# A retention, mixing and gated-MLP kernel: whole-tile first loads, a seven-product last layer and a re-searched order

## The chip, the cores and the metric

One core of one Trainium2 chip. The metric is device time in microseconds (us); an interval is given where runs were repeated. Span means the time from the first to the last instruction in the profile. The engines are TensorE (PE), VectorE (DVE), ScalarE (ACT), GpSimd (POOL) and SyncE (SP), which mainly issues transfers.

## What is computed

Three blocks follow one another on an array of 2 batches x 768 tokens x 512 features, all in float32:

```
attention: state[t] = gamma_h * state[t-1] + k[t] v[t]^T ;  y[t] = q[t] state[t] / 8     (8 heads of 64)
mixing:    theta = x @ w_theta
           u = x + w_tok_r @ (x cos theta) + w_tok_i @ (x sin theta)          (over tokens)
           x = u + relu(u @ w_ch)
gated MLP: h = gelu(x @ w_in) ;  u, v = halves of h
           v = (w_sg @ layernorm(v) * g_ln) + b_sg                             (over tokens)
           out = x + (u * v) @ w_out
```

## The kernel before, in words

**Numbers.** A float32 product is made of three passes in PE's faster type fp32r: each operand is split into a high part (ACT, line 324) and a low part (DVE, line 330), and `terms3` (line 345) issues high x high, low x high and high x low into one accumulator. A 128 x 512 tile with a contraction of 512 is thus 4 x 3 = 12 matmuls of 512 columns. Only the attention runs in plain float32.

**Tiles.** The 768 tokens of a batch are six chunks of 128; chunk i = 0 to 11 counts over both batches. From the mixing on, tokens stand in three groups of 512: group 0 is batch 0's first 512 tokens, group 1 is batch 1's, group 2 the last 256 tokens of both. Features stand in four row tiles of 128. A tile is called (group, row tile).

**Loads.** `load_half` (line 439) brings a chunk in two halves of 512 KB (q with k, and k with v). For chunk 0 each half goes in two transfers of 64 partitions, one on SP's queue and one on ACT's; all others go whole on SP's. From chunk 3 on, a load waits for the attention of the chunk three before (`gate`, line 441). Behind chunk 0's halves SP issues `dec` (line 467), 262 KB: the decay factors `dq` by which the attention's result is multiplied, and the small ones `dk` and `gone` for the keys and the state. Weights come in 1 MB transfers and are converted on ACT and DVE (`weight`, line 371).

**Attention** (`retention`, line 460): scores, a mask on DVE, a fade of v by `dk` (on ACT, eight small instructions, for the first eight chunks; else one on DVE), an outer product for the next state, the attention product, and the multiplication by `dq` on DVE.

**Last layers.** `gate_tile(g, f)` (line 961) makes the products over tokens, an affine step on DVE (line 998), a multiplication by u (line 1005), and the split into `ghl[g, f]`. `finish(g, d)` (line 1013) makes the product with `w_out` by `layer` (12 matmuls), adds x in the evacuation (line 1020) and stores. The last tile, (2, 3), is done in two halves of 256 columns (line 1057). There are 12 such tiles, 8 of them in groups 0 and 1.

**Order.** Every instruction group is an `Op` with a modelled duration, and `ORDER` (line 168) is a list found by an offline search. `Plan.schedule` (line 112) walks it with a model of the engines' and queues' times, gives out buffers and PSUM banks, and sorts by modelled start. Each engine runs its instructions in that order; a modelled gap of PE in the first 34 us is filled with matmuls on the identity (`keep_warm`, line 1137), and eight matmuls on a zeroed state come first of all.

Of the kernel before, what the change touches and what calls it, by code (L numbers as in the profile page):

```python
# [10 lines left out]
F32 = mybir.dt.float32  # L11
# [51 lines left out]
class Plan:  # L63
# [3 lines left out]
    BEGIN = {"PE": 4.9, "ACT": 2.3, "DVE": 1.4, "POOL": 2.0, "SP": 0.8, "SPA": 0.8}  # L67
    FLY = 8
# [37 lines left out]
    def switch(self, a, b):  # L106
        tiled = ("scores", "outer", "attend")
        if a in ("main", "turn") and b in tiled:
            return 0.09 if a == "main" else 0.23
        return {"attend": 0.09 * (b != "outer"), "outer": 0.07}.get(a, 0.0) * (a != b)  # L110

    def schedule(self, order):
# [8 lines left out]
        landed, last = [], {}  # L121
        for o in (self.ops[k] for k in order):
# [7 lines left out]
            if o.eng == "SP" and len(landed) >= self.FLY:  # L130
                t = max(t, landed[-self.FLY])
            for b in o.bufs:
                if b.base is None:
                    room = free[b.of]
                    b.base = min(range(len(room)), key=lambda k: room[k])
                    t = max(t, room[b.base] + 0.1)
                    room[b.base] = math.inf
            o.start, o.end = t, t + o.dur
            if o.eng in ("SP", "SPA"):
                engines[o.eng] = t + 0.45  # L140
                if sent < t + 1.25:
                    sent = t + 1.75
                    if t > 20:
                        behind = 0.4
# [4 lines left out]
                if o.eng == "SP":  # L149
                    landed.append(o.end)  # L150
# [68 lines left out]
def retention_spectral_gmlp(  # L219
# [5 lines left out]
    decays: bass.AP,  # L225
    gvec: bass.AP,
# [34 lines left out]

    ident = const.tile([P, P], F32, name="ident")
# [16 lines left out]
    dec = const.tile([P, 512 + H + NP], F32, name="dec")  # L279
    dq, dk, gone = dec[:, 0:512], dec[:, 512 : 512 + H], dec[:, 512 + H :]  # L280
    grown = const.tile([P, NP * D], F32, name="grown")
    states = [const.tile([P, NP * D], F32, name=f"state{n}") for n in range(2)]
    V.memset(states[0], 0.0)
# [19 lines left out]
    def mm(o, l, r, start, stop):  # L303
        nc.tensor.matmul(out=o, lhsT=l, rhs=r, start=start, stop=stop)  # L304
# [40 lines left out]
    def terms3(o, terms, start=True, stop=True):  # L345
        n = len(terms)
        for i, ((lh, ll), (rh, rl)) in enumerate(terms):
            mm(o, lh, rh, start and i == 0, False)
            mm(o, ll, rh, False, False)
            mm(o, lh, rl, False, stop and i == n - 1)  # L350
# [12 lines left out]
    wp = {}  # L363
# [7 lines left out]
    def weight(k, prio, eng=dve, after=()):  # L371
# [53 lines left out]
        f = lambda: words(0).bitcast(F32)  # L425
        split_hi(lambda: ap(h, F32R), f, 1024, prio, [(raw, 0), *keys], w=[h])
# [9 lines left out]

    load = {}

    def load_half(i, k):
        b, c = divmod(i, NCH)  # L440
        x = load[i, k] = Buf("pair")

        def rows(queue, a, e):
            queue.dma_start(out=ap(x)[a:e], in_=qkv[b, c, k][a:e])  # L444
# [8 lines left out]
    def landed(x):  # L453
        return [(x, "top"), (x, "low")]
# [777 lines left out]
```

## Time and profile before

| | us |
|---|---|
| median of 3 runs (375.22 to 375.40) | 375.26 |
| the profiled execution | 375.16 |
| its span | 373.4 |
| PE busy in the span | 366.1 (98%) |
| DVE busy | 267.6 (72%) |
| ACT busy | 171.8 (46%) |

The profile is of one execution. Busy times are sums over instructions; a PE that is "busy" can still run below its peak, since matmuls overlap and their ends are modelled. What counts for the time is which wait ends last in each stage.

### The profile page before, as it was taken

The page shows a single profiled execution, that of the slowest core. Times are in us where ns is not written, and L with a number is a line of the kernel's source. Part 1 is how long each engine was busy: PE and PEld are TensorE (multiplying, and loading weights), DVE is VectorE, ACT ScalarE, POOL GpSimd, SP SyncE. Part 2 cuts the span into 40 slices and gives each one's busy share as a digit, 9 for nine tenths or more (in the row PEclk, how much of TensorE's full clock was granted, in tenths as well). Part 3 has the DMA queues.
Part 4 walks back from the last instruction along what each step waited for, and adds up shares of the span by engine and source line. Part 5 has one row for each costly group of instructions (what it writes and reads, how often), then busy time and mean ns, then how long its engine had stood idle before and what let it go on. Part 6 is the DMA issues. An engine that isn't in the chain of part 4 may idle for free.

```text
span 373.4 us, 5719 instructions
## 1 busy us (share of the span) xinstructions
PE 366.1 (98%) x2372; PEld 314.1 (84%) x2372; DVE 267.6 (72%) x408; ACT 171.8 (46%) x292; POOL 11.0 (3%) x18
## 2 busy tenths in 40 slices
PE   7899999999999999999999999999999999999996
PEld 6788888888899888889988888888888888899885
DVE  1898999979887998646478237985989795542453
ACT  2877786755462576413344026427466813000010
POOL 1101002000000300000000000000000000000000
PEclk9999999999999999999999999999999999999999
DMA  7999904255438100442042000000000000000124
GB/s 214 416 409 412 366 31 145 64 216 198 168 119 326 64 0 11 190 126 100 2 149 104 2 0 0 2 0 1 2 0 0 1 2 0 30 0 2 56 85 169
DMA packets 10234, 39.04 MB, mean 105 GB/s; under 512 B 1248, under 2 KB 2272, under 8 KB 7776
## 3 DMA queue, kind: packets, MB, share of 16 engines
q1 hardware_dynamic: 10048, 38.15, 27.3%
q10 hardware_dynamic: 160, 0.52, 0.6%
q8 instruction: 18, 0.29, 0.3%
q14 instruction: 8, 0.07, 0.1%
HBM read 35.53 MB, written 3.15 MB: 104 GB/s over the span
## 4 chain that ended last, share of the span: by engine, by line
PE 94%; DMA 5%; ACTq 0%; DVE 0%; issue 0%
PE banks L304 93%; DMA b<-qkv 5%; PE banks L678 1%; ACTq L444 0%; DVE b L1057 0%
## 5 line engine op out<-in xcount | busy, mean ns | idle before, releaser
L304 PE MATMUL banks<-b,b 128*128 128x512 f32 (+2 forms) x1788 | 330.2, 351 | 0.0
L304 PEld LDWEIGHTS banks<-b,b 128*128 128x128 f32 (+1 forms) x1788 | 278.3, 183 | 46.4 <-issue 1.0
L324 ACT ACTIVATE b<-b 128x512 fp32r<-128x512 f32 (+1 forms) x61 | 50.2, 846 | 79.2 <-DVE b L1005 44.7
L330 DVE TENSOR_TENSOR b<-b,b 128x512 fp32r<-128x512 f32 (+1 forms) x61 | 56.0, 932 | 16.1 <-ACT b L324 11.9
L416 DVE SCALAR_TENSOR_TENSOR b<-b 128x1024 int32<-128x1024 int32 x32 | 39.1, 1221 | 5.0 <-ACT b L396 4.9
L819 ACT ACTIVATE b<-banks 128x512 f32<-128x512 f32 x24 | 13.5, 589 | 30.9 <-PE banks L304 30.9
L827 DVE SCALAR_TENSOR_TENSOR b<-b,banks 128x512 f32<-128x512 f32 x24 | 16.1, 682 | 15.4 <-ACT b L819 15.4
L324 ACT ACTIVATE b<-xa 128x512 fp32r<-128x512 f32 (+1 forms) x26 | 17.1, 668 | 15.3 <-DVE xa L729 8.3
L304 PE MATMUL banks<-b 64*128 64x128 f32 (+1 forms) x352 | 19.8, 261 | 2.5 <-DMA b<-qkv 2.5
L304 PEld LDWEIGHTS banks<-b 64*128 64x128 f32 (+1 forms) x352 | 17.8, 170 | 4.8 <-DMA b<-qkv 3.4
L484 DVE TENSOR_TENSOR b<-banks,causal 128x512 f32<-128x512 f32 x24 | 15.6, 684 | 8.3 <-PE banks L304 8.3
L330 DVE TENSOR_TENSOR b<-xa,b 128x512 fp32r<-128x512 f32 (+1 forms) x26 | 18.7, 730 | 2.7 <-ACT b L324 2.7
L396 ACT ACTIVATE b<-b 128x1024 f32<-128x1024 f32 x16 | 18.5, 1153 | 3.1 <-DMA b<-wts 3.1
L837 ACT ACTIVATE b<-b 128x512 f32<-128x512 f32 x24 | 14.6, 626 | 10.4 <-DVE b L827 10.3
L502 ACT ACTIVATE b<-b,dec 128x64 f32<-128x64 f32 x64 | 16.1, 336 | 5.7 <-DMA dec<-decays 5.1
L998 DVE SCALAR_TENSOR_TENSOR b<-banks,gcol,brow 128x512 f32<-128x512 f32 x12 | 8.9, 747 | 13.2 <-PE banks L304 13.2
L843 DVE SCALAR_TENSOR_TENSOR b<-b,banks 128x512 f32<-128x512 f32 x24 | 16.1, 678 | 3.0 <-ACT b L837 2.9
L686 DVE TENSOR_TENSOR b<-banks,b 128x1024 f32<-128x1024 f32 x12 | 14.5, 1219 | 0.4 <-ACT b L669 0.4
L1020 DVE TENSOR_TENSOR b<-banks,xa 128x512 f32<-128x512 f32 x8 | 5.5, 689 | 13.0 <-PE banks L304 13.0
L324 ACT ACTIVATE b<-xb 128x512 fp32r<-128x512 f32 (+1 forms) x13 | 8.4, 664 | 12.6 <-DVE xb L765 9.3
L928 ACT ACTIVATE b<-b,rstd 128x512 f32<-128x512 f32 x12 | 9.6, 806 | 7.9 <-DVE rstd L917 7.9
L634 ACT ACTIVATE b<-banks 128x512 int32<-128x512 f32 x12 | 7.1, 592 | 10.9 <-PE banks L304 10.9
(58 smaller groups left out, 179.4 us busy)
## 6 DMA issues: line engine op xcount, KB each, us to landing
b<-wts SPq DMA_DIRECT2D x16, 1024.0 KB, 4.9
b<-qkv SPq DMA_DIRECT2D x22, 512.0 KB, 10.8
out<-b SPq DMA_DIRECT2D x11, 256.0 KB, 2.4
b<-wsg SPq DMA_DIRECT2D x9, 256.0 KB, 5.5
xa<-wts SPq DMA_DIRECT2D x2, 1024.0 KB, 11.8
xb<-wts SPq DMA_DIRECT2D x1, 1024.0 KB, 9.5
b<-qkv ACTq DMA_DIRECT2D x2, 256.0 KB, 4.3
b<-qkv SPq DMA_DIRECT2D x2, 256.0 KB, 5.5
```

The lines of the kernel that those rows point to most:

```text
L304: nc.tensor.matmul(out=o, lhsT=l, rhs=r, start=start, stop=stop)
L324: act(words, lambda: A.activation(out=hi(), in_=src(), func=AF.Copy), prio=prio, r=r, **k)
L330: lambda: E.tensor_tensor(out=lo(), in0=src(), in1=hi().bitcast(F32), op=ALU.subtract),
L396: lambda: A.activation(out=words(1).bitcast(F32), in_=words(1).bitcast(F32), func=AF.Copy, scale=REBIAS),
L416: lambda scalar=scalar, op=op: V.scalar_tensor_tensor(out=words(0), in0=words(1), scalar=scalar, in1=words(0), op0=op, op1=ALU.bitwise_or,),
L484: V.tensor_tensor(out=ap(at[i])[:, h * 512 : (h + 1) * 512].rearrange("p (n t) -> p n t", n=NP), in0=ap(sc[h]).rearrange("p (n t) -> p n t ...
L502: A.activation(out=v, in_=v, func=AF.Copy, scale=dk[:, h : h + 1])
L686: V.tensor_tensor(out=z2, in0=ap(tp)[:, None, :].to_broadcast([P, 2, 512]), in1=z2, op=ALU.mult)
L819: lambda: A.activation(out=ap(s), in_=ap(t), func=AF.Square),
L827: lambda: V.scalar_tensor_tensor(out=ap(s), in0=ap(s), scalar=1.0 / GA, in1=ap(t), op0=ALU.add, op1=ALU.mult),
L837: lambda: A.activation(out=ap(s), in_=ap(s), func=AF.Tanh, scale=GA * GC),
L843: lambda: V.scalar_tensor_tensor(out=ap(o), in0=ap(s), scalar=1.0, in1=ap(t), op0=ALU.add, op1=ALU.mult),
```

## The change

**Loads.** Chunk 0's halves are loaded as the others, in one transfer of 128 partitions each on SP's queue. The table is cut in two: `dk` and `gone`, padded to 96 columns (48 KB), go on ACT's queue; `dq` (256 KB) goes on SP's. In DRAM and in the tile the halves' columns are regrouped by pairs of heads; instruction counts and sizes of the attention stay. The fade of chunk 0 moves to DVE. The wait of a load for the attention three chunks before is gone.

**Last layer.** The 8 tiles of groups 0 and 1 are one product of 2 x 2 blocks: A11, A12, A21, A22 are 256 x 256 blocks of `w_out`, transposed, and B11, B12, B21, B22 blocks of the gated activations (first index: feature half; second: batch). Winograd's form needs seven products of blocks with sums of the operands: of the weights S1 = A21 + A22, S2 = S1 - A11, S3 = A11 - A21, S4 = A12 - S2, and of the activations T1 = B12 - B11, T2 = B22 - T1, T3 = B22 - B12, T4 = B21 - T2. `seven` runs once per 128 rows of a block (j = 0, 1): seven products of 6 matmuls into four PSUM banks, `finish_four` adds and stores four tiles.

**Order.** `ORDER` is new (935 entries in place of 884). The gates now run (0,3), (0,2), (0,0), (0,1), the four of group 2, then (1,1), (1,3), (1,2), (1,0). Behind them PE does, with round j in brackets: A11 B11 [0]; tiles (2,0) and (2,2); S1 T1 [0]; tile (2,1); S2 T2 [0]; S1 T1 [1]; A12 B21 [0]; S3 T3 [0]; A11 B11 [1]; A22 T4 [0]; S2 T2 [1]; S3 T3 [1]; S4 B22 [0]; A12 B21 [1]; A22 T4 [1]; S4 B22 [1]; the two halves of (2,3). Up to the first theta product PE does the same work as before (scores of chunks 0 to 3, outer products and attention of 0 to 2). SP's queue begins: both halves of chunks 0 and 1, `dq`, the first theta weight, chunks 2 and 3, the vector `gvec`, the second theta weight, chunks 4 and 5, a `wsg` tile, the second and the first main weight, chunk 6's second half, chunk 7, chunk 10's first half, chunk 8's and chunk 6's first halves. Before, it began: chunk 0, `dec`, chunk 1, the first theta weight, chunks 2 and 3, the second theta weight, chunk 4, a `wsg` tile, chunk 5, the first main weight, chunk 6.

**The rest.** The planner's constants change, six matmuls on the zeroed state in place of eight, that state's memset first, and gaps of PE in the first 9 us filled from 0.4 us on in place of 0.8.

```diff
     def load_half(i, k):
         x = load[i, k] = Buf("pair")
-        t = dict(prio=early(i) - 12 + k, after=[gate[i - 3]] if i >= 3 else ())
-        if i == 0:
-            dma(256, lambda: rows(nc.sync, 0, 64), w=[(x, "top")], **t)
-            dma(256, lambda: rows(nc.scalar, 64, P), eng="SPA", w=[(x, "low")], **t)
-        else:
-            dma(512, lambda: rows(nc.sync, 0, P), w=[(x, "top"), (x, "low")], **t)
+        dma(
...
+            lambda: nc.sync.dma_start(out=ap(x), in_=qkv[b, c, k]),
...
         if i == 0:
-            dma(264, lambda: nc.sync.dma_start(out=dec, in_=decays), w=["dk"], prio=t - 10.9)
+            dma(48, lambda: nc.scalar.dma_start(out=dec, in_=decays), eng="SPA", w=["dk"], prio=t - 10.9)
+            dma(256, lambda: nc.sync.dma_start(out=dq, in_=qdecays), w=["dq"], prio=t - 10.9)
...
-        if i < C["FA"]:
+            if 0 < i < C["FA"]:
                 plan.op("ACT", 2.01, fade_v_heads, **k)
...
-        ghl[g, f] = pair()
-        split(ghl[g, f], lambda: ap(m), 512, prio, [m])
+        if g != 1 or f >= 2:
+            ghl[g, f] = pair()
+            split(ghl[g, f], lambda: ap(gu[g, f]), 512, prio, [gu[g, f]])
+
+    def sum_weights(base, prio):
...
+        for i, (x, y, op, of) in enumerate(pairs):
+            dve(
+                512,
+                lambda i=i, x=x, y=y, op=op: V.tensor_tensor(out=s3(i), in0=x(), in1=y(), op=op),
...
+            split(res[i], lambda i=i: ap(sums[i]), 512, prio, [sums[i]])
...
+    def sum_tokens(src, prio):
...
+            sums = [(b12, b11), (b22, own[0]), (b22, b12), (b21, own[1])]
+            for i, ((x, kx), (y, ky)) in enumerate(sums):
+                dve(
...
+                split(res[i, n], lambda i=i, t=t: ap(t[i]), 512, prio, [t[i]])
...
+    def seven(base, src, hl, ws, ts, j, prio):
+
+        z, w, x, y = (bank() for _ in range(4))
...
+        def product(o, a, b, first):
+            tile, keys = a
+
+            def products():
+                terms = [(tile(n), tuple(ap(v, F32R) for v in b[n])) for n in range(2)]
+                terms3(ap(o), terms, first, True, not first)
+
+            pe(1.36, products, r=[*keys, *b[0], *b[1]], w=[o], prio=prio)
...
+        product(z, a_of(0, 0), b_of(0, 0), True)
+        product(w, s_of(1), t_of(1), True)
+        both(u, z, w)
+        product(x, s_of(0), t_of(0), True)
+        product(y, s_of(2), t_of(2), True)
+        both(v, x, y)
+        product(z, a_of(0, 1), b_of(0, 1), False)
+        product(x, s_of(3), b_of(1, 1), False)
+        product(y, a_of(1, 1), t_of(3), False)
+        return z, x, y, u, v
...
+    def finish_four(j, ws, ts, prio):
+        z, x, y, u, v = seven(W_OUT, None, ghl, ws, ts, j, prio)
...
+        add(o, lambda: ap(z), lambda: x_tile(0, j), [z, *x_keys(0, j)], ps=True)
+        store(0, j, o, prio)
+        for g, d, part in ((1, j, x), (0, 2 + j, y)):
+            o = Buf()
+            add(o, lambda: ap(u), lambda g=g, d=d: x_tile(g, d), [u, *x_keys(g, d)])
+            add(o, lambda part=part: ap(part), lambda o=o: ap(o), [part], ps=True)
+            store(g, d, o, prio)
+        add(v, lambda: ap(u), lambda: ap(v), [u])
+        add(v, lambda: ap(v), lambda: x_tile(1, 2 + j), x_keys(1, 2 + j))
+        store(1, 2 + j, v, prio)
```

`both(o, a, b)` copies accumulator a to SBUF on ACT and adds accumulator b to it on DVE, ahead of the later products into the same banks.

## Rows read from the trace of the kernel before

**Rows 1.** Page, part 1: busy us (share of span) and instructions by engine.

```profile
PE 366.1 (98%) x2372; PEld 314.1 (84%) x2372; DVE 267.6 (72%) x408; ACT 171.8 (46%) x292; POOL 11.0 (3%) x18
```

**Rows 2.** Waits of PE, whole execution: who waited for whom: us, times, longest.

```profile
PE banks L304 <- DMA b<-qkv: 2.5, 3, 1.3
PE banks L304 <- DVE state L283: 1.3, 1, 1.3
```

**Rows 3.** Windows: stretch, length, busy us (instructions) by engine, PEclk, DMA share, GB/s.

```profile
2.00:5.00 3.00, 3.00 (x15) 2.75 (x13) 0.00 (x0) 1.28 (x1) 0.00 (x0) 1.00 1.01 249
5.00:7.50 2.50, 2.15 (x20) 1.98 (x20) 0.16 (x1) 0.00 (x0) 0.00 (x0) 1.00 0.99 204
7.50:18.60 11.10, 8.56 (x142) 7.21 (x140) 8.54 (x14) 8.88 (x27) 1.52 (x1) 1.00 1.04 417
20.00:40.00 20.00, 20.00 (x256) 16.71 (x252) 18.05 (x26) 15.95 (x44) 1.84 (x3) 1.00 1.02 409
20.00:370.00 350.00, 350.00 (x2184) 300.08 (x2178) 256.77 (x391) 160.88 (x263) 8.34 (x9) 1.00 0.24 92
300.00:340.00 40.00, 40.00 (x228) 35.30 (x227) 23.71 (x36) 6.89 (x11) 0.00 (x0) 1.00 0.02 7
300.00:370.00 70.00, 70.00 (x389) 61.33 (x387) 37.09 (x57) 9.21 (x15) 0.00 (x0) 1.00 0.11 38
```

**Rows 4.** The chain that ended last: start us, us, what.

```profile
6.55 11.99 DMA b<-qkv
18.59 11.84 PE banks L304 x146
...
143.70 226.59 PE banks L304 x1146
```

**Rows 5.** Timeline of DVE, last 10 us: start us, us, instruction [idle before, releaser].

```profile
364.72 0.69 DVE L1020 TENSOR_TENSOR b<-banks,xb 128x512 f32<-128x512 f32 x1 [4.75 <-PE banks L304]
365.33 0.68 DVE L1020 TENSOR_TENSOR b<-banks,xa 128x512 f32<-128x512 f32 x1
365.93 0.68 DVE L1020 TENSOR_TENSOR b<-banks,xb 128x512 f32<-128x512 f32 x1
...
367.44 0.69 DVE L1020 TENSOR_TENSOR b<-banks,xb 128x512 f32<-128x512 f32 x1 [0.83 <-PE banks L304]
```

**Rows 6.** Groups by line and shape, DVE and ACT: busy us, mean ns, idle before.

```profile
L330 DVE TENSOR_TENSOR b<-b,b 128x512 fp32r<-128x512 f32 x33 | 22.1, 685 | 2.3 <-ACT b L324 2.2
L998 DVE SCALAR_TENSOR_TENSOR b<-banks,gcol,brow 128x512 f32<-128x512 f32 x12 | 8.9, 747 | 13.2 <-PE banks L304 13.2
...
L324 ACT ACTIVATE b<-b 128x512 fp32r<-128x512 f32 x33 | 19.6, 623 | 44.9 <-DVE b L1005 44.7
```

**Rows 7.** Transfers from 2 to 3 us: 40 slices, and the only data queue.

```profile
GB/s 0 0 0 0 164 492 328 328 164 164 0 328 655 655 328 328 164 164 0 328 328 0 0 328 0 0 0 0 0 0 0 164 492 328 164 0 0 164 819 983
...
q10 hardware_dynamic: 51, 0.21, 87.9%
```

**Rows 8.** Timeline of the head, as rows 5.

```profile
0.78 1.20 ACTq L444 DMA_DIRECT2D b<-qkv  x2
...
0.78 1.46 SPq L444 DMA_DIRECT2D b<-qkv  x2
...
8.43 2.02 ACT L502 ACTIVATE b<-b,dec 128x64 f32<-128x64 f32 x8 [5.14 <-DMA dec<-decays]
...
18.59 1.16 PE L304 MATMUL banks<-b 64*128 64x128 f32 x16 [0.87 <-DMA b<-qkv]
...
19.68 1.09 PE L304 MATMUL banks<-b,state 64*64 64x128 f32 x16
```

**Rows 9.** Timeline of PE around a transpose, as rows 5.

```profile
28.75 1.69 PE L304 MATMUL banks<-b,b 128*128 128x512 f32 x6
30.27 0.60 PE L678 MATMUL banks<-ident,xa 128*128 128x128 f32 x4
30.62 2.99 PE L304 MATMUL banks<-b,b 128*128 128x512 f32 x12
```

**Rows 10.** Groups by line and shape, PE, as rows 6.

```profile
L304 PE MATMUL banks<-b,b 128*128 128x512 f32 x1140 | 263.1, 391 | 0.0
```

More of the change, by code (lines that the diff above doesn't have):

```diff
@@ L120, in schedule @@
         behind, form = 0.45, None
-        landed, last = [], {}
+        landed, last, made = [], {}, {}
         for o in (self.ops[k] for k in order):
@@ L140, in schedule @@
                 engines[o.eng] = t + 0.45
[L141 to L144, printed above, removed]
+                made[o.eng] = max(made.get(o.eng, 0.0), t) + 1.0
+                if sent < t + 1.25 and t > 20:
+                    behind = 0.4
+                sent = max(sent, made[o.eng] + 0.75)
                 if sent + o.dur > 15 and sent < 20:
@@ L148, in schedule @@
                 o.end = sent + behind
-                if o.eng == "SP":
-                    landed.append(o.end)
+                landed.append(o.end)
             else:
@@ L259, in halves @@
         return Half(b, 0), Half(b, 1)
+    states = [const.tile([P, NP * D], F32, name=f"state{n}") for n in range(2)]
+    V.memset(states[0], 0.0)
     ident = const.tile([P, P], F32, name="ident")
@@ L278, in retention_spectral_gmlp @@
     )
-    dec = const.tile([P, 512 + H + NP], F32, name="dec")
-    dq, dk, gone = dec[:, 0:512], dec[:, 512 : 512 + H], dec[:, 512 + H :]
+    dec = const.tile([P, 96], F32, name="dec")
+    dk, gone = dec[:, 0:H], dec[:, H : H + NP]
+    dq = const.tile([P, 512], F32, name="dq")
     grown = const.tile([P, NP * D], F32, name="grown")
-    states = [const.tile([P, NP * D], F32, name=f"state{n}") for n in range(2)]
-    V.memset(states[0], 0.0)
     xa = [const.tile([P, NP, TA], F32, name=f"xa{b}") for b in range(B)]
@@ L300, in x_keys, with mm @@
         return [("x", b, c, d) for b in range(B) for c in range(TA // P, NCH)]
-    def mm(o, l, r, start, stop):
-        nc.tensor.matmul(out=o, lhsT=l, rhs=r, start=start, stop=stop)
+    def mm(o, l, r, start, stop, more=False):
+        nc.tensor.matmul(out=o, lhsT=l, rhs=r, start=start, stop=stop, skip_group_check=more)
     def pe(dur, fn, **k):
@@ L441, in load_half, with landed, part_of @@
         x = load[i, k] = Buf("pair")
-        def rows(queue, a, e):
-            queue.dma_start(out=ap(x)[a:e], in_=qkv[b, c, k][a:e])
-        t = dict(prio=early(i) - 12 + k, after=[gate[i - 3]] if i >= 3 else ())
-        if i == 0:
-            dma(256, lambda: rows(nc.sync, 0, 64), w=[(x, "top")], **t)
-            dma(256, lambda: rows(nc.scalar, 64, P), eng="SPA", w=[(x, "low")], **t)
-        else:
-            dma(512, lambda: rows(nc.sync, 0, P), w=[(x, "top"), (x, "low")], **t)
-    def landed(x):
-        return [(x, "top"), (x, "low")]
-    gate = {}
+        dma(
+            512,
+            lambda: nc.sync.dma_start(out=ap(x), in_=qkv[b, c, k]),
+            w=landed(x),
+            prio=early(i) - 12 + k,
+        )
+    def landed(x, pairs=range(NP)):
+        return [(x, g) for g in sorted({p // 2 for p in pairs})]
+    def part_of(x, second, p):
+        c = (p // 2) * 512 + second * 256 + (p % 2) * P
+        return ap(x)[:, c : c + P]
     xhl, at = {}, {}
@@ L493, in fade_v, with scores, mask @@
-        def fade_v():
-            v3 = ap(kv)[:, 512:1024].rearrange("p (h d) -> p h d", h=H)
-            V.tensor_tensor(
-                out=v3, in0=v3, in1=dk[:, :, None].to_broadcast([P, H, D]), op=ALU.mult
-            )
+        at[i] = Buf("pair")
+        for pairs in steps:
+            lo, hi = pairs[0] * P, (pairs[-1] + 1) * P
+            def scores(pairs=pairs):
+                for p in pairs:
+                    for h in range(2):
+                        rows = slice(h * D, (h + 1) * D)
+                        cols = slice(p * P, (p + 1) * P)
+                        q, k = part_of(qk, 0, p), part_of(qk, 1, p)
+                        mm(ap(sc[h])[:, cols], k[rows], q[rows], True, True)
+            pe(
+                1.09 / share, scores, form="scores", r=landed(qk, pairs),
+                w=[(sc[h], pairs[0]) for h in range(2)], prio=t,
+            )
+            for h in range(2):
+                def mask(h=h, lo=lo, hi=hi, n=len(pairs)):
+                    V.tensor_tensor(
+                        out=ap(at[i])[:, h * 512 + lo : h * 512 + hi].rearrange(
+                            "p (n t) -> p n t", n=n
+                        ),
+                        in0=ap(sc[h])[:, lo:hi].rearrange("p (n t) -> p n t", n=n),
+                        in1=causal[:, None, :].to_broadcast([P, n, P]),
+                        op=ALU.mult,
+                    )
+                dve(
+                    512 // share, mask, ps=True, r=[(sc[h], pairs[0])], w=[(at[i], h, pairs[0])],
+                    prio=t + 1,
+                )
@@ L509, in retention, with faded @@
+        def faded(pairs=range(NP)):
+            return [*landed(kv, pairs), *((kv, "v", g) for _, g in landed(kv, pairs))]
         state, state_next = states[c % 2], states[(c + 1) % 2]
@@ L564, in attend @@
                         )
-            for p in range(NP):
+            for p in pairs:
                 cols = slice(p * P, (p + 1) * P)
@@ L575, in attend @@
                     )
-        r = [*landed(kv), (kv, 1), (at[i], 0), (at[i], 1)]
-        if c > 0:
-            r += [*landed(qk), ("state", c % 2)]
-        gate[i] = pe(0.93 if c == 0 else 1.95, attend, form="attend", r=r, w=[xp], prio=t + 3)
+        for pairs in steps:
+            r = [*faded(pairs), (at[i], 0, pairs[0]), (at[i], 1, pairs[0])]
+            if c > 0:
+                r += [*landed(qk), ("state", c % 2)]
+            pe(
+                (0.93 if c == 0 else 1.95) / share, named(attend, pairs),
+                form="attend", r=r, w=[(xp, pairs[0])], prio=t + 3,
+            )
         keys = [("x", b, c, d) for d in range(NP)]
@@ new lines, in sum_weights, with block, s3 @@
+    def sum_weights(base, prio):
+        def block(e, k):
+            return plain[base + k][0]().rearrange("p (n e) -> p n e", n=2)[
+                :, :, e * 256 : (e + 1) * 256
+            ]
+        res = []
+        sums = [*halves(), *halves()]
+        def s3(i):
+            return ap(sums[i]).rearrange("p (n e) -> p n e", n=2)
+        pairs = [
+            (lambda: block(1, 0), lambda: block(1, 1), ALU.add, []),
+            (lambda: s3(0), lambda: block(0, 0), ALU.subtract, [0]),
+            (lambda: block(0, 0), lambda: block(1, 0), ALU.subtract, []),
+            (lambda: block(0, 1), lambda: s3(1), ALU.subtract, [1]),
+        ]
+        for i, (x, y, op, of) in enumerate(pairs):
+            dve(
+                512,
+                lambda i=i, x=x, y=y, op=op: V.tensor_tensor(out=s3(i), in0=x(), in1=y(), op=op),
+                r=[plain[base][1], plain[base + 1][1], *(sums[n] for n in of)],
+                w=[sums[i]],
+                prio=prio,
+            )
+            res.append(pair())
+            split(res[i], lambda i=i: ap(sums[i]), 512, prio, [sums[i]])
+        return res
@@ new lines, in sum_tokens @@
+    def sum_tokens(src, prio):
+        res = {}
+        for n in range(2):
+            t = [Buf() for _ in range(4)]
+            b11, b12, b21, b22 = (src(g, d) for d in (n, 2 + n) for g in range(2))
+            own = [(lambda x=x: ap(x), [x]) for x in t]
+            sums = [(b12, b11), (b22, own[0]), (b22, b12), (b21, own[1])]
+            for i, ((x, kx), (y, ky)) in enumerate(sums):
+                dve(
+                    512,
+                    lambda o=t[i], x=x, y=y: V.tensor_tensor(
+                        out=ap(o), in0=x(), in1=y(), op=ALU.subtract
+                    ),
+                    r=[*kx, *ky],
+                    w=[t[i]],
+                    prio=prio,
+                )
+                res[i, n] = pair()
+                split(res[i, n], lambda i=i, t=t: ap(t[i]), 512, prio, [t[i]])
+        return res
@@ new lines, in seven, with a_of, s_of, tile @@
+    def seven(base, src, hl, ws, ts, j, prio):
+        z, w, x, y = (bank() for _ in range(4))
+        def a_of(e, k):
+            cols = slice(e * 256 + j * P, e * 256 + (j + 1) * P)
+            return lambda n: tuple(v[:, cols] for v in w_tile(base + k, n)), [*wp[base + k]]
+        def s_of(i):
+            def tile(n):
+                return tuple(
+                    ap(v, F32R)[:, n * 256 + j * P : n * 256 + (j + 1) * P] for v in ws[i]
+                )
+            return tile, [*ws[i]]
+        def product(o, a, b, first):
[4 more added lines that the diff above has]
+            pe(1.36, products, r=[*keys, *b[0], *b[1]], w=[o], prio=prio)
+        def b_of(g, k):
+            return [hl[g, 2 * k + n] for n in range(2)]
+        def t_of(i):
+            return [ts[i, n] for n in range(2)]
+        def both(o, a, b):
+            act(
+                512, lambda: A.activation(out=ap(o), in_=ap(a), func=AF.Copy), ps=True,
+                r=[a], w=[o], prio=prio,
+            )
+            dve(
+                512,
+                lambda: V.tensor_tensor(out=ap(o), in0=ap(b), in1=ap(o), op=ALU.add),
+                ps=True, r=[b], w=[o], prio=prio,
+            )
+        u, v = Buf(), Buf()
+        product(z, a_of(0, 0), b_of(0, 0), True)
[8 more added lines that the diff above has]
+        return z, x, y, u, v
@@ L1122, in retention_spectral_gmlp @@
         weight(W_OUT + k, t + 20 + 5 * k)
-    for g in range(3):
+    for g in (2, 0, 1):
         for f in range(NP):
@@ L1213 @@
     )
+    dk, dq = _decays()
     arrays = {
```

161 lines of the change are left out of this document (94 added, 67 removed), and 94 rows, old and new, of the table ORDER.

## The prediction

> **What bounds the kernel now.** Read the page's busy shares first [rows 1]: TensorE (PE) is busy for 366.1 of 373.4 us, VectorE (DVE) for 267.6. Then ask what PE ever waited for [rows 2]: 2.5 us for chunk loads and 1.3 us for the first memset, all of it early: in the stretch from 20 to 370 us PE is busy for 350.00 of 350.00 [rows 3]. The chain of waits says the same from the other side [rows 4]: transfers of `qkv` up to 18.55 us, then PE without a break to 370.29, then 3.1 us of evacuation and last store. So the time is (a) the moment at which PE's unbroken run begins, set by the loads, (b) the length of that run, set by the number of matmuls, (c) a tail of 3.1 us. DVE is nearly full in the front half (18.05 of 20 us from 20 to 40) and loose at the back (23.7 of 40 from 300 to 340) [rows 3]. The profiled execution took 375.16 us, 1.76 beyond its span and 0.10 under the median of 375.26; the sum is made against 375.16.
>
> **Part 1, the last layer: 12 matmuls fewer.** Eight output tiles (two batches' first 512 tokens, four row tiles) of 12 matmuls each, 96, become two rounds of seven products of 6, 84. The price is in the last tiles: the evacuation of tile (2,1) starts when PE frees it at 364.72, that of (2,2) at 367.44 [rows 5]: 2.72 us per 12 matmuls of 512 columns, 0.227 each. Saved: 12 x 0.227 = **2.72 us**, all of it on the path, since PE is the path there.
>
> What it adds stands on DVE and ScalarE (ACT). DVE: 4 weight sums, 8 token sums, 12 low parts of their splits, less 2 splits no longer made, and 18 additions at the output in place of 8: 32 instructions of 0.69 us by themselves [rows 6], 0.60 apart when they follow on each other (365.33 to 365.93 [rows 5]); I use 0.62, so 20 us. ACT: 10 high parts of 0.62 us [rows 6] and 4 copies, 9 us. The cover: from 300 to 370 us DVE now works for 37 of 70 us, ACT for 9 [rows 3]. So in bulk it fits; what has to be checked is the chain behind the last gate tile, (1,0), whose product all four sums over the first token block contain.
>
> Call the end of that gate's matmuls G. By the order in the diff PE then does product Z (1.36), tiles (2,0) and (2,2) (2.72 each), and needs T1 at G+6.8. DVE does in order: affine, the second sum of the other block, two gate products, two sums, the two low parts of T1: 0.2 (PE's lag) + 0.75 [rows 6] + 7 x 0.62 = G+5.3. Slack 1.5. Next PE does that product and tile (2,1) and needs T2 and S2 at G+10.9; DVE has seven more instructions, G+9.7. Slack 1.2. Then three products on data that is there, and T3 at G+15.0: six more DVE instructions, one of which waits for PE's second product at G+12.4, G+13.7. Slack 1.2. The tightest place is the accumulator Y of round 0, which PE must not add to before DVE has read it: DVE is through at G+17.2, PE arrives at G+17.7. I cost all this at nothing; without that cover PE waits us for us. The reads and writes in place on the PSUM banks add waits of the same kind only (a bank of round 1 must be evacuated first), with more slack.
>
> **Part 2, the head.** Chunk 0 comes today in four transfers of 64 rows over two queues, then a table of 262 KB; afterwards in two transfers of 128 rows on SyncE's queue (SP), with a 48 KB table on ACT's queue and the rest of the table, 256 KB, moved behind chunk 1. Bytes and order up to the fourth chunk are otherwise the same, so what can change is the rate. The windows [rows 3]: 249 GB/s from 2 to 5 us and 204 from 5 to 7.5, then 417 up to 18.6. The engines' busy share is about 1 throughout; only the yield is half. The 3.0 x 0.249 + 2.5 x 0.204 = 1.26 MB moved by 7.5 us are about chunk 0 and the table (1,024 + 262 KB, 1.32 MB): the slow stretch ends where the 64-row transfers and the table end. At the later 0.417 MB/us they take 3.0 us. When would the stream start? ACT's first issue moved its first bytes at 2.1 (the fifth of 40 slices), and from 2 to 3 us ACT's queue (q10) alone moved anything [rows 7]: SP's first bytes come after 3.0, although issued at the same 0.78 [rows 8]. So the 1.26 MB are through between 5.1 and 6.0 in place of 7.5: a gain of 1.5 to 2.4 us. The first load will stand on SP, so I go a third of the way up, **1.8 us**. Bound below: 0, if the rate is slow because the stream is young.
>
> Does it reach PE? The run begins with the attention of the third chunk at 19.68, straight behind the scores of the fourth, which waited for their load at 18.59 [rows 8]; transfers are saturated up to there, so every load and with it these two move forward by the same. DVE is busy for 8.5 of the 11.1 us up to there [rows 3], but its work hangs on the table: the fade of chunk 0 waited 5.1 us for it on ACT, until 8.43, and took 2.02 [rows 8]. Now one DVE instruction of 512 elements, 0.69 [rows 6], does it on a table that lands with the first load; DVE's chain moves by over 2 us and does not take over.
>
> **Part 3, order.** From the first theta product on, PE changes over to transposes or back 22 times in place of 20. A six-matmul half begun at 28.75 ends at 30.11, the transposes start at 30.27 and the next product 0.35 later [rows 9]: 0.16 per change-over, **+0.3 us** for two. Loads no longer wait for the attention three chunks before, which can only bring them forward. SP's queue is also reordered: chunk 6's first half now stands behind two 1 MB weights and its own other half and four halves of later chunks. By bytes it is 14.2 MB into the stream: 2.65 (SP's start as taken above) + 14.2/0.41 + 1 to 2 us of lag (an estimate: the fourth chunk's first half, 5.0 MB in, would by this land at 7.5 + 3.8/0.417 = 16.6, and landed at 18.55) = 38 to 39. PE gets there after eight theta halves (8 x 1.36), four scores (1.09 each [rows 8]), three attentions (an estimate of twice that each, with twice the matmuls) and 1.5 us of outer products and change-overs, at 19.68 - 1.8 + 23 = 41. Covered by 2 us. Six warming matmuls for eight and finer filling of gaps lie ahead of the first load: nothing, bounds 0 to 0.2.
>
> **Part 4, the tail.** The last tile is still halved; 3.1 us stay; the stores of the tile before now go out two small tiles earlier, 0 to -0.3, taken 0.
>
> **Sum.** 375.16 - 2.72 - 1.8 + 0.3 = 370.94; on the scale of the median 371.04, said as **371.0**.
>
> **Rivals.**
> *The head gives nothing.* Mechanism: the first 5 us of a stream are slow whatever its shape, or PE's own start takes over. Against it: 204 GB/s from 5 to 7.5 and 417 after it, a step at the place where the shapes change, not a ramp [rows 3]. For it: all the early bytes are such shapes, so no row shows a whole transfer early. 375.16 - 2.72 + 0.3 = 372.7. Chance 0.15. [...]
> *PE waits for the sums (the other side).* Place: DVE behind the last gate. Price: if DVE is B us behind when that gate ends, PE waits B - 1.2; from B = 6.2 on (ten instructions) all 4.2 us of gain and 0.75 more are gone. If the eight instructions of the other token block and four of the weights' are still queued, B = 7.4: 371.0 + 6.2 = 377.2. For it: DVE executes in order, and 13 of these instructions are placed among the gates' own. Against: 23.7 of 40 us busy before, some 32 then. Slower 0.08; a part of it (0.5 to 3 us, 371.5 to 374.0) 0.07; just even 0.05.
> *More than forecast.* SP's stream starts at 2.1 and the change-overs cost nothing: 375.16 - 2.72 - 2.4 = 370.0; with some tenths of hidden gaps in the 350 us closed, 369.5. Chance 0.05.
> *It doesn't do what it says.* Counted in the diff: 14 products of 6 matmuls for 8 tiles of 12; the work is really gone, no chance given.
>
> **How the numbers follow.** Forecast 0.60 (370.0 to 371.9), the others as above. A measurement of this kernel tells about 0.2% (0.75 us) from no change. Faster: 0.60 + 0.15 + 0.07 + 0.05 = 0.87; same 0.05; slower 0.08. The range has to take in both ends of the head (370.0 to 372.7), the tenths on either side and half of the small waits: 369.6 to 373.3.
>
> **What would show it.** Matmuls of 512 columns: 1128 in place of 1140 [rows 10]; DVE 33 instructions more (the 32 and chunk 0's fade). The window from 3 to 7.5 us at about 400 GB/s; scores of the fourth chunk near 16.8. No wait of PE after 20 us; in the last 30 us none on DVE or ACT. Wrong: 200 GB/s before 7.5 us still, a new line of PE waits in the list, or a run that begins early but ends late.

## The result and the profile after

370.30 us median (370.23 to 370.63, four runs) against 375.33 (375.22 to 375.41, four runs): a ratio of 0.9869, 95% interval 0.9855 to 0.9883, or 5.0 us less. Forecast were 371.0 and a range of 369.6 to 373.3. The profiled execution took 370.23 us with a span of 368.5.

The page's first part, as [rows 1]: PE has 8 instructions less in all (12 matmuls fewer in the last layer; of the matmuls that fill PE's gaps, 4 less on the zeroed state and 8 more on the identity), DVE the 33 more that the prediction counted, and 22.5 us more work.

```profile
PE 363.0 (99%) x2364; PEld 311.7 (85%) x2364; DVE 290.1 (79%) x441; ACT 178.6 (48%) x298; POOL 10.8 (3%) x18
```

PE's waits in the whole execution, as [rows 2]. The loads' share fell from 2.5 us to 0.8, and no new line has come in: the sums of the seven products are never waited for. The kernel before had the third line too:

```profile
PE banks L678 <- DVE xa L584: 0.4, 1, 0.4
```

and after:

```profile
PE banks L311 <- DVE halfpi L273: 1.2, 1, 1.2
PE banks L311 <- DMA b<-qkv: 0.8, 2, 0.6
PE banks L716 <- DVE xa L622: 0.2, 1, 0.2
```

The windows, as [rows 3]: length, busy us of PE, its weight loads, DVE, ACT, POOL, granted clock, share of the DMA engines, GB/s. The last column of the first two lines is the head's story (249 and 204 before); the DVE column of the fourth, 34.02 of 40 (23.71 before), is cover that has been used up, some 6 us of it by the last layer: the run with eight tiles below, in the same order up to the gates, has 27.76 there.

```profile
2.00:5.00 3.00, 3.00 (x19) 2.88 (x19) 0.00 (x0) 0.49 (x1) 0.00 (x0) 1.00 0.90 330
5.00:7.50 2.50, 2.44 (x40) 2.06 (x40) 1.59 (x3) 0.00 (x0) 0.00 (x0) 1.00 1.03 419
...
20.00:40.00 20.00, 20.00 (x204) 16.62 (x204) 19.31 (x27) 15.07 (x37) 2.56 (x3) 1.00 1.03 410
300.00:340.00 40.00, 40.00 (x245) 36.06 (x245) 34.02 (x54) 13.27 (x23) 0.00 (x0) 1.00 0.01 1
```

The chain that ended last, as [rows 4]. Loads end their part of it 2.0 us earlier, and from there PE never breaks off until 130.49 + 234.79 = 365.28.

```profile
5.12 11.40 DMA b<-qkv
...
16.56 30.70 PE banks L311 x384
...
130.49 234.79 PE banks L311 x1188
```

These lines split the 4.9 us of span. The run of PE begins 18.59 - 16.56 = 2.03 us earlier; it lasts 365.28 - 16.56 = 348.72 us in place of 351.70, 2.98 less; the tail is 3.22 in place of 3.11. Sum: 2.03 + 2.98 - 0.11 = 4.90.

The 2.98 can be split again. Behind the last transposes only products are left. Counted at the prices of the last layer's own rows, 2.72 for 12 matmuls of 512 columns [rows 5] and 1.44 for 12 of 256 (363.87 to 365.30 below), the stretch from there should take 226.48 us before (834 matmuls of 512 columns and 312 of 256) and 234.72 after (864 and 324); it took 226.59 [rows 4] and 234.79. PE runs at its price to within 0.1 us over 230. What is left of the attention, transposes and change-overs ahead of it, products taken off at the same prices, is 38.47 us before and 38.25 after.

The timeline of DVE at the end, as [rows 5]: the last outputs are added while PE still works, and the two halves of the last tile are waited for from PE as before.

```profile
360.32 1.29 DVE L1180 TENSOR_TENSOR b<-b,xa 128x512 f32<-128x512 f32 x2
361.52 0.69 DVE L1180 TENSOR_TENSOR b<-banks,b 128x512 f32<-128x512 f32 x1
362.43 0.69 DVE L1180 TENSOR_TENSOR b<-banks,b 128x512 f32<-128x512 f32 x1 [0.22 <-PE banks L311]
363.87 0.42 DVE L1231 TENSOR_TENSOR b<-banks,xb 128x256 f32<-128x256 f32 x1 [0.74 <-PE banks L311]
365.30 0.42 DVE L1231 TENSOR_TENSOR b<-banks,xb 128x256 f32<-128x256 f32 x1 [1.01 <-PE banks L311]
```

### The profile page after: what moved, and what is told of

The parts are those of the page before. It is cut to its first block, busy times and chain, and to the rows that moved or that the text cites. A ratio compares the mean times of both kernels' runs of the same rounds, so it can differ in the third digit from the quotient of the medians.

```text
span 368.5 us, 5764 instructions
## 1 busy us (share of the span) xinstructions
PE 363.0 (99%) x2364; PEld 311.7 (85%) x2364; DVE 290.1 (79%) x441; ACT 178.6 (48%) x298; POOL 10.8 (3%) x18
## 4 chain that ended last, share of the span: by engine, by line
PE 95%; DMA 4%; DVE 0%; SPq 0%; issue 0%
PE banks L311 93%; DMA b<-qkv 3%; PE banks L716 1%; DMA dec<-decays 1%; DVE b L1231 0%; SPq L457 0%
## 5 line engine op out<-in xcount | busy, mean ns | idle before, releaser
L331 ACT ACTIVATE b<-b 128x512 fp32r<-128x512 f32 (+1 forms) x71 | 56.0, 815 | 67.4 <-DVE b L423 23.5
L337 DVE TENSOR_TENSOR b<-b,b 128x512 fp32r<-128x512 f32 (+1 forms) x71 | 62.4, 898 | 15.4 <-ACT b L331 9.2
L526 ACT ACTIVATE b<-b,dec 128x64 f32<-128x64 f32 x56 | 14.1, 335 | 7.4 <-DMA b<-qkv 7.4
L412 DVE TENSOR_SCALAR b<-b 128x1024 int32<-128x1024 int32 x16 | 11.4, 717 | 4.2 <-DMA b<-wts 4.2
L845 DVE SCALAR_TENSOR_TENSOR xa<-banks,xa 128x512 f32<-128x512 f32 x8 | 5.5, 690 | 8.0 <-PE banks L311 7.9
L311 PE MATMUL banks<-b,state 64*64 64x128 f32 x160 | 10.9, 275 | 0.0
```

The costliest lines, as they stand in the source:

```text
L331: act(words, lambda: A.activation(out=hi(), in_=src(), func=AF.Copy), prio=prio, r=r, **k)
L337: lambda: E.tensor_tensor(out=lo(), in0=src(), in1=hi().bitcast(F32), op=ALU.subtract),
L526: A.activation(out=v, in_=v, func=AF.Copy, scale=dk[:, h : h + 1])
```

## The experiments

Theory: the time fell by two independent terms, the rate of the first transfers (2.0 us) and 12 matmuls (2.7 us), each worth its full size because PE waits for nothing else. Rivals: the head's gain comes of the table, of the queues or of the new order; the sums of the last layer are not free; change-overs of PE have a price.

### The new loading alone, in the kernel of before

```diff
-        if i == 0:
-            dma(256, lambda: rows(nc.sync, 0, 64), w=[(x, "top")], **t)
-            dma(256, lambda: rows(nc.scalar, 64, P), eng="SPA", w=[(x, "low")], **t)
-        else:
-            dma(512, lambda: rows(nc.sync, 0, P), w=[(x, "top"), (x, "low")], **t)
+        dma(512, lambda: rows(nc.sync, 0, P), w=[(x, "top"), (x, "low")], **t)
...
-            dma(264, lambda: nc.sync.dma_start(out=dec, in_=decays), w=["dk"], prio=t - 10.9)
+            dma(48, lambda: nc.scalar.dma_start(out=dec, in_=decays), eng="SPA", w=["dk"], prio=t - 10.9)
+            dma(256, lambda: nc.sync.dma_start(out=dq, in_=qdecays), w=["dq"], prio=t - 10.9)
...
-        if i < C["FA"]:
+        if 0 < i < C["FA"]:
...
```

The last line moves the fade of chunk 0 to DVE, as in the changed kernel; the order of the other instructions is that of before.

> The kernel before with the new loading of chunk 0 and of the table alone (order otherwise that of before). Theory (shape): the first 1.26 MB move at about 410 GB/s in place of 228, scores of the fourth chunk start near 16.6 in place of 18.59, and the time falls by 1.8 to 2.1 us to 373.2 to 373.5. Rival (the head's gain needs the new order, or a young stream is slow): scores of the fourth chunk no earlier than 18.0, time above 374.6.

373.29 us (373.26 to 373.82) against 375.36: ratio 0.9951, interval 0.9935 to 0.9968, 2.1 us less. The first two windows:

```profile
2.00:5.00 3.00, 3.00 (x17) 2.77 (x15) 0.00 (x0) 0.50 (x1) 0.00 (x0) 1.00 0.86 325
5.00:7.50 2.50, 2.19 (x27) 1.88 (x28) 1.64 (x3) 0.00 (x0) 0.00 (x0) 1.00 1.03 419
```

and in its timeline the scores of the fourth chunk, which began at 18.59 [rows 8]:

```profile
16.63 1.16 PE L306 MATMUL banks<-b 64*128 64x128 f32 x16 [0.75 <-DMA b<-qkv]
```

The loading by itself, under the old order, gives all of the head's gain.

### The halves of 64 rows again, on two queues and on one

In the changed kernel; the split table stays.

```diff
-        dma(
...
-            lambda: nc.sync.dma_start(out=ap(x), in_=qkv[b, c, k]),
...
+        if i == 0:
+            dma(256, lambda: rows(nc.sync, 0, 64), w=[(x, 0), (x, 1)], **t)
+            dma(256, lambda: rows(nc.scalar, 64, P), eng="SPA", w=[(x, "low")], **t)
+        else:
+            dma(512, lambda: rows(nc.sync, 0, P), w=landed(x), **t)
...
```

For one queue the line of the lower rows has `nc.sync` and `eng="SP"`.

> The changed kernel with chunk 0 again in four transfers of 64 rows, two on SyncE's and two on ScalarE's queue; the split table stays. Shape: the stretch from 2.5 to 7 us falls back to 200 to 250 GB/s, the fourth chunk's scores start 1.2 to 1.6 us later (17.8 to 18.2), time 371.5 to 371.9; the old table makes up the rest of the 2.0. Rival (it was the table that was slow, not the halves): 370.2 to 370.6.

> As the kernel with four transfers of 64 rows, but all four on SyncE's queue, upper and lower rows in turn. If the number of rows makes the rate: again 200 to 250 GB/s and 371.5 to 371.9 or slower, since only one half of the partitions is written at a time. If two queues side by side were the trouble: about 400 GB/s and 370.2 to 370.6.

373.07 us on two queues (373.02 and 373.11), 373.02 on one (372.97 and 373.07). The first two windows, of the kernel with two queues:

```profile
2.00:5.00 3.00, 3.00 (x18) 3.00 (x17) 0.00 (x0) 1.28 (x1) 0.00 (x0) 1.00 1.02 258
5.00:7.50 2.50, 2.40 (x26) 1.96 (x24) 0.00 (x0) 0.00 (x0) 0.00 (x0) 1.00 1.05 256
```

and of the one with one queue:

```profile
2.00:5.00 3.00, 3.00 (x16) 3.00 (x15) 0.00 (x0) 0.47 (x1) 0.00 (x0) 1.00 1.01 242
5.00:7.50 2.50, 2.50 (x21) 2.28 (x21) 0.00 (x0) 0.00 (x0) 0.00 (x0) 1.00 1.03 231
```

In these runs the rate went with the number of rows: whole transfers 419 GB/s in the second window, halves 231 to 256, whether they shared a queue or not, at the same busy share of about 1. It isn't the size of 256 KB: `dq`, as large but in 128 rows, landed some 0.65 us behind the load ahead of it in the changed kernel, about 0.4 MB/us. A young stream is not slow as such (the changed kernel moves 414 GB/s from 3 to 5 us): the rival "the head gives nothing" falls. But 2.8 us is about twice the 1.2 to 1.6 expected. The windows account for a part: 0.257 or 0.237 MB/us for 5.5 us against 0.371 leaves 0.6 to 0.7 MB, some 1.6 us. The rest stands in the timelines of PE. The changed kernel has

```profile
14.15 1.78 PE L311 MATMUL banks<-b 64*128 64x128 f32 x32 [0.16 <-DMA b<-qkv]
16.56 1.16 PE L311 MATMUL banks<-b 64*128 64x128 f32 x16 [0.64 <-DMA b<-qkv]
17.65 1.09 PE L311 MATMUL banks<-b,state 64*64 64x128 f32 x16
```

and the one with halves on two queues

```profile
17.40 1.78 PE L312 MATMUL banks<-b 64*128 64x128 f32 x32 [0.66 <-DMA b<-qkv]
19.52 1.16 PE L312 MATMUL banks<-b 64*128 64x128 f32 x16
20.61 1.09 PE L312 MATMUL banks<-b,state 64*64 64x128 f32 x16
```

The last load that PE waits for is now the third chunk's, at 17.40, and not the fourth's, at 16.56: 0.84 us later, but with 3.21 us of PE's matmuls between it and the third chunk's attention, where the changed kernel has 1.09. So this attention starts 2.96 us later; the run with one queue has 17.38 and 20.60. That load is there 3.25 us later than in the changed kernel (14.15). Its forerunner landed 2.1 us later, 14.9 against 12.8; the rest is a wide gap between landings: of the loads of 512 KB around here most land about 1.3 us apart, but one lands 2.4 to 2.8 behind its forerunner. In the kernel before and in the changed one that is the fourth chunk's, here the third's. Why there is such a gap no run shows.

### The table in one piece

```diff
-            dma(48, lambda: nc.scalar.dma_start(out=dec, in_=decays), eng="SPA", w=["dk"], prio=t - 10.9)
-            dma(256, lambda: nc.sync.dma_start(out=dq, in_=qdecays), w=["dq"], prio=t - 10.9)
+            dma(264, lambda: nc.sync.dma_start(out=dec, in_=decays), w=["dk", "dq"], prio=t - 10.9)
...
```

The whole table stands behind chunk 0, as in the kernel before, and no longer behind chunk 1.

> The changed kernel with whole transfers of chunk 0, but the table in one piece of 262 KB on SyncE's queue behind chunk 0. Shape of rows (2,096 bytes, an odd piece of 48 at the end of each): the 0.27 MB move at about 190 GB/s and cost 0.5 to 0.8 us, time 370.8 to 371.1. Rival (only the halves were slow, and the table's place is covered): within 0.2 of 370.3. Rival (the fade behind the late table becomes the bound): more than 371.3.

370.82 us (370.78 and 370.86): half a us, as expected; what is due to the rate and what to the table's place is not told apart. Its second window moves 335 GB/s, between the 419 of the changed kernel and the 231 to 256 of the halves:

```profile
5.00:7.50 2.50, 2.16 (x24) 1.85 (x24) 0.19 (x1) 0.00 (x0) 0.00 (x0) 1.00 1.01 335
```

So, undone one by one, the halves are the larger part of the head and the table the smaller.

### The whole old loading under the new order

Both edits above together:

```diff
-        dma(
...
-            lambda: nc.sync.dma_start(out=ap(x), in_=qkv[b, c, k]),
...
+        if i == 0:
+            dma(256, lambda: rows(nc.sync, 0, 64), w=[(x, 0), (x, 1)], **t)
+            dma(256, lambda: rows(nc.scalar, 64, P), eng="SPA", w=[(x, "low")], **t)
...
-            dma(48, lambda: nc.scalar.dma_start(out=dec, in_=decays), eng="SPA", w=["dk"], prio=t - 10.9)
-            dma(256, lambda: nc.sync.dma_start(out=dq, in_=qdecays), w=["dq"], prio=t - 10.9)
+            dma(264, lambda: nc.sync.dma_start(out=dec, in_=decays), w=["dk", "dq"], prio=t - 10.9)
...
```

> The changed kernel with the whole loading of before (four transfers of 64 rows on two queues, table of 262 KB in one piece on SyncE's queue behind them), the new order and last layer kept. With whole transfers restored in the kernel of before the loading was worth 2.1; undoing the halves alone here cost 2.8. If the loading is worth the same under either order: 370.3 + 2.1 = 372.4 (372.2 to 372.7), and the excess in the run with halves comes from the small table going out beside them. If the new order leans more on early loads: 372.9 to 373.6.

372.87 us (372.49 and 373.24), 2.6 us over the changed kernel. This falls between the two expectations, and its two runs lie on either side. It is clear that 2.8 for the halves and 0.5 for the table don't add up: together they cost no more than the halves alone. The timeline shows why: here too PE waits for the third chunk's load last, until 17.23, and its attention starts at 20.03, 2.38 us later than in the changed kernel. The same loading under the old order has the fourth chunk's load last and this attention at 19.68 [rows 8], 0.35 earlier.

### Eight tiles in place of seven products

```diff
-        if g != 1 or f >= 2:
-            ghl[g, f] = pair()
-            split(ghl[g, f], lambda: ap(gu[g, f]), 512, prio, [gu[g, f]])
+        ghl[g, f] = pair()
+        split(ghl[g, f], lambda: ap(gu[g, f]), 512, prio, [gu[g, f]])
...
-    for j in range(2):
-        finish_four(j, ws, ts, t)
-        t += 10
...
+    for g in (2, 0, 1):
+        for d in range(NP):
+            finish(g, d, t)
```

> The changed kernel with the eight tiles of groups 0 and 1 made by twelve matmuls each, as before; head, order up to the gates and all else as changed. Theory: the seven products are worth their 12 matmuls of 0.227 us, no less and no more: 370.3 + 2.7 = 373.0 (372.7 to 373.3), with no wait of PE at the end of either. Rival (the sums cost something, or the freed DVE time shortens the end): less than 372.5.

373.07 us (373.05 to 373.08, four runs), 2.77 more. In the chain of waits the stretch behind the last transposes takes 237.51 us for 1200 matmuls, where the changed kernel has 234.79 for 1188: 2.72 us for 12.

```profile
130.66 237.51 PE banks L309 x1200
```

The seven products are worth their matmuls exactly; the 19.6 us of further DVE work (290.1 us against 270.5) cost nothing.

### How much cover is left behind the last gate

```diff
+    for _ in range(4):
+        dve(
...
+            lambda: V.tensor_tensor(out=dq, in0=brow[:, 0:512], in1=brow[:, 0:512], op=ALU.add),
...
```

These stand in the order right behind the last gate's affine step; `dq` is no longer read there.

> The changed kernel with four more DVE instructions of 0.69 us (a sum that nothing uses) right behind the affine step of the last gate, ahead of the token sums. Theory (slack of 1.1 to 1.25 us behind the last gate, read in the changed kernel's timeline): DVE runs 2.4 us later, PE waits 1.2 to 1.4 us in all, time 371.4 to 371.7. Rival (more cover than that): 370.2 to 370.6. Rival (no cover, every us counts): 372.7.

> The same with twelve such instructions: 7.2 to 7.4 us later, less 1.1 to 1.25 of cover, PE waits 6.0 to 6.3 us, time 376.3 to 376.6, over that of the kernel before: the rival on the other side with its price. If DVE catches up elsewhere: below 375.3.

One run each. With four, 371.77: 1.5 us more. With twelve, 377.86: 7.6 us more, well over the kernel before. The added instructions follow on each other at 0.72 us in place of the 0.60 I had used (8.67 for twelve, below), so four are 2.9 us and twelve 8.7. Four cost 1.5 of 2.9: the cover is 1.4, against 1.2 in the prediction (or 1.5, since this execution's unbroken run also began 0.2 us later, at 16.73). Twelve show something else besides. First the timeline (DVE's added work, then PE's wait):

```profile
335.87 8.67 DVE L1306 TENSOR_TENSOR dq<-brow 128x512 f32<-128x512 f32 x12
...
347.85 25.08 PE L312 MATMUL banks<-b,b 128*128 128x512 f32 x114 [5.89 <-ACT b L332]
```

PE waited 5.9 us, not 7.6, and once, for T1's high part. So the cover at that place is 8.7 - 5.9 = 2.8 us; with four, where the cover is 1.4, the chain's last wait ends at a later sum, at 347.77. The windows of the same kernel (the third figure from the end is the granted clock) have the rest:

```profile
342.00:344.00 2.00, 0.00 (x0) 0.00 (x0) 1.90 (x4) 0.00 (x0) 0.00 (x0) 1.00 0.00 0
344.00:346.00 2.00, 0.00 (x0) 0.00 (x0) 2.00 (x4) 0.23 (x1) 0.00 (x0) 0.58 0.00 0
346.00:348.00 2.00, 0.15 (x1) 0.16 (x1) 1.81 (x4) 1.73 (x4) 0.00 (x0) 0.50 0.00 0
348.00:350.00 2.00, 2.00 (x5) 1.57 (x6) 2.00 (x4) 1.35 (x3) 0.00 (x0) 0.50 0.00 0
350.00:352.00 2.00, 2.00 (x8) 1.54 (x8) 2.00 (x4) 1.04 (x2) 0.00 (x0) 0.71 0.00 0
352.00:354.00 2.00, 2.00 (x10) 1.68 (x9) 2.00 (x5) 1.12 (x3) 0.00 (x0) 1.00 0.40 135
```

While PE stood still the granted clock fell to 0.50, and the windows from 348 to 352 count 5 and 8 matmuls, where the next, at 1.00, counts 10. Short of full clock are 2.15 us x 0.50 from 347.85 to 350 and 2.00 x 0.29 up to 352, in all 1.7. This long wait of PE cost itself and that: 5.9 + 1.7 = 7.6. Waits for the later sums did not come on top: the 114 matmuls behind it take 25.08 us, 1.8 over their price. With four's cover of 1.4, and no fall of the clock, 8.7 - 1.4 = 7.3 us of waiting would be expected (an estimate, not run), so the fall by itself cost some 0.3.

### Where the small table goes

On SP's queue, behind the first load and ahead of the next three, in place of ACT's:

```diff
-            dma(48, lambda: nc.scalar.dma_start(out=dec, in_=decays), eng="SPA", w=["dk"], prio=t - 10.9)
+            dma(48, lambda: nc.sync.dma_start(out=dec, in_=decays), w=["dk"], prio=t - 10.9)
```

> The changed kernel with the small table (48 KB) on SyncE's queue behind the first load, nothing on ScalarE's queue. In the changed kernel the first us of the stream (2 to 3 us) moves only 164 GB/s while the table's 384-byte rows go beside the first load. If the table on its own queue is what slows that us: the first load and all behind it 0.2 to 0.4 us earlier, time 369.9 to 370.1. If the start is slow by itself: within 0.2 of 370.3. If the fade of chunk 0 then waits: later.

371.84 us (eight runs, 371.59 to 374.61): slower by 1.5 and less steady. The expectation was wrong in an instructive way. The first us is faster, 336 GB/s, but the next two carry 172 (the changed kernel has 164 and 414):

```profile
2.00:3.00 1.00, 1.00 (x7) 1.00 (x6) 0.00 (x0) 0.06 (x1) 0.00 (x0) 1.00 0.96 336
3.00:5.00 2.00, 2.00 (x11) 2.00 (x11) 0.00 (x0) 0.00 (x0) 0.00 (x0) 1.00 0.78 172
```

Here these 128 rows of 384 bytes, ahead of the 512 KB transfers in one queue, held up what was behind them (172 GB/s from 3 to 5 us); beside them, on ACT's queue in the changed kernel, they did not (414).

Two attempts to beat the changed kernel followed: the same table on ACT's queue behind that engine's function table load, meant to come 1.3 us later,

```diff
-        if o.eng == "ACT" and not loaded:
+        if o.eng in ("ACT", "SPA") and not loaded:
```

> The changed kernel with the small table issued on ScalarE's queue behind that engine's function table load, about 1.3 us later. The run with the table on SyncE's queue showed 336 GB/s from 2 to 3 us with nothing beside the first load, against 164 with the table there. If the table's start is what slows the first load's: 0.17 MB or 0.4 us ahead from 3 us on, the fourth chunk's scores near 16.2, time 369.8 to 370.1. If its 128 small rows cost the stream the same wherever they come: within 0.2 of 370.3. If the fade of chunk 0 then waits for the table and that is not covered: up to 371.3.

and with rows of 512 bytes.

```diff
-    dec = const.tile([P, 96], F32, name="dec")
+    dec = const.tile([P, 128], F32, name="dec")
...
```

> The changed kernel with the small table padded to 128 columns, rows of 512 bytes in place of 384 (some later small tiles take its unused columns). If rows under 512 bytes are handled slower: the first us of the stream moves more than 164 GB/s and the time falls by 0.1 to 0.4 to 369.9 to 370.2. If it is the number of rows, not their size: within 0.2 of 370.3.

370.52 (370.40 to 370.92) and 370.37 (369.98 to 370.63): neither differs from 370.30. The first edit did not do what it was for. The function table load began first, but the table's transfer was issued at 0.81, where the changed kernel has 0.78, so a later table is untested:

```profile
0.78 1.28 ACT L1332 ACT_TABLE_LOAD   x1 [0.78 <-PEq L1407]
0.81 0.39 ACTq L481 DMA_DIRECT2D dec<-decays  x1
```

In the second, PE no longer waits for any load; its list of waits is down to the memset and one tile of DVE:

```profile
PE banks L311 <- DVE halfpi L273: 1.2, 1, 1.2
PE banks L716 <- DVE xa L622: 0.2, 1, 0.2
```

This need not be the work of the wider rows: three runs with the changed kernel's own loading (eight tiles, twelve late, paired groups) have no wait for a load either. In all four the wide gap between landings falls one load later, so the fourth chunk's first half is there at 15.3 to 15.4 and not at 16.5. The third chunk's attention behind it starts at 18.04 in this run and at 17.82, 17.64 and 17.30 in the three others, where the changed kernel has 17.65: there the head hangs on PE's and DVE's own chain. A load 1.2 us earlier moved the start by no more than 0.4 us to either side, so the next us in the head is not to be had from this load.

### Change-overs between products and transposes

Only the order is edited: three transpose groups (133, 214 and 316 in the list) are moved up or down to stand beside another. One of the three:

```diff
-    29, 105, 206, 182, 79, 106, 133, 30,
+    29, 105, 133, 206, 182, 79, 106, 30,
```

> The changed kernel with three pairs of transpose groups moved next to each other (of chunks 1 and 2, 5 and 8, 7 and 10): six change-overs between products and transposes fewer, no work changed. By the prediction's price of 0.16 us each: 1.0 us faster, 369.3. By the chain of waits, where a group standing alone and two side by side take 0.44 us each: no change, 370.1 to 370.5.

370.33 us (369.81 to 370.43): no change. In the chain a pair of groups takes 1.02 us (x8), where the changed kernel has them apart, 0.59 and 0.44:

```profile
46.89 1.02 PE banks L717 x8
```

```profile
47.26 0.59 PE banks L716 x4
47.85 1.39 PE banks L311 x6
49.24 0.44 PE banks L716 x4
```

From the third chunk's attention to the end of the last transposes the two kernels differ by less than 0.1 us (17.30 to 130.09 and 17.65 to 130.49). Here a change-over has no price of its own (1.02 us against 1.03).

## Why the prediction was right, and where not

**What bounds the kernel: right.** PE's unbroken run, a head set by loads and a tail of 3.1 us were the whole time before, and they are after (in four of the other traces the head ends on PE's and DVE's own chain, as shown above).

**Part 1, 12 matmuls: right to the hundredth.** 2.72 forecast, 2.72 in the chain and 2.77 in the medians by the run with eight tiles. The cover was priced by adding up DVE's instructions behind the last gate; the added instructions measured it at 1.4 us against 1.2, in one run. The rival on the other side was right in kind: its point is real, twelve instructions late make the change a loss. Its price came out, 7.5 us for B = 8.7 against 7.6, but not by its mechanism: there were 5.9 of waiting, since at T1 the cover was 2.8 and not 1.5, and 1.7 short of full clock (0.50 to 0.71 was granted), which it left out. That the two make up for each other is luck.

**Part 2, the head: right in size, its inside only in part.** 1.8 forecast, 2.03 in the trace, 2.1 by the loading alone. The step "SP's first bytes come after 3.0" did not carry over: SP's queue moved bytes from 1.8 on, but only 164 GB/s from 2 to 3 us, which comes to nearly the same as the start at 2.65 that I took: that was luck. And the start of the third chunk's attention varies, 17.30 to 17.82 in four other traces with the same loading, so agreement to 0.2 us says little. What I had argued from the place of the step in the rate (it ends where the 64-row transfers end) the runs with halves have shown.

Halves and whole transfers are not equal in bandwidth here: 231 to 256 GB/s against 419 from 5 to 7.5 us, at a busy share of about 1 in all three runs. Why a transfer of 64 rows moves little more than half of that, and why two queues side by side stay at 256, no run here shows.

**Part 3, order: wrong.** The term of +0.3 us for two more change-overs failed; the stretch that holds them became 0.2 us shorter (38.47 to 38.25). I had read one gap of 0.16 us in front of one group [rows 9] as a price per change-over. The chain of the kernel before holds the answer in its groups of four and of eight (0.44 and 0.88 us), and the run with paired groups shows it: nothing. The 0.2 us that went the other way are not explained; they are more than traces of one order differ by over this stretch (113.93 and 113.92 us from the fourth chunk's scores on in two with the new order, 125.11 and 125.13 in two with the old). The rest of the part held: chunk 6's late load was covered, no wait of PE after 20 us.

**Part 4, the tail.** 3.22 against 3.11; forecast as equal.

**Open.** Why one load of the stream lands 2.4 to 2.8 us behind its forerunner, and what decides which one it is; on that hangs how much of the old loading's cost reaches PE (2.6 us under the new order, 2.1 under the old one). The 0.7 us between forecast and result are the head (0.2) and the order (0.3 not lost, 0.2 to 0.3 gained), less 0.1 of tail.

## What to carry to other kernels

Where one engine is busy from the first loads to the last store, price a change in that engine's instructions and check the cover of everything else instruction by instruction behind the point where it comes free; both were good to 0.3 us here. Look at the yield of the first transfers, not at their busy share: GB/s by window shows a shape that wastes almost half of it (here 231 to 256 against 419, at busy shares of 1.03 to 1.05). A price per event must come from a view that varies the number of events, not from one gap.

## What was not expected of the hardware

A small table in a queue held up what was behind it far beyond its bytes: 48 KB in rows of 384 bytes ahead of 512 KB transfers cut two us of the stream to 172 GB/s (the stream had 414 there) and cost 1.5 us against the same table on the other queue. Whether the size of its rows does this is not shown; rows of 512 bytes were tried on the other queue alone. And in a wait of 5.9 us by PE the granted clock fell to 0.5; the first four us behind it ran at 0.5 to 0.7, 1.7 us short of full clock.
